# Attention and a mixture of experts on one core: stores on GpSimd's queue, and seven smaller edits

## The chip, the core and the metric

The kernel runs on one core of a Trainium2 chip. A core has a matrix engine (TensorE, PE in the profile, with its weight loads as PEld), a vector engine (VectorE, DVE), an engine for activations and copies (ScalarE, ACT), GpSimd (POOL) and SyncE (SP), which here only issues DMAs. Each engine works through its own instructions in order and waits for the others at semaphores; a "q" behind an engine's name (POOLq) means its sequencer. Sixteen DMA engines move data between the device memory and the core's own memory. The metric is the device time of one execution in microseconds (us).

## What is computed

The first half is sparse attention over 8 batches, 8 heads, 576 positions and 64 columns a head. The second half sends each of the 4,608 rows through one of 8 experts.

```python
# attention: heads 0-3 see the last 32 positions, heads 4-7 see positions of their own class mod 32
scores = scale * np.matmul(q, k.transpose(0, 1, 3, 2))
...
scores = np.where(masks[None, :, :, :], scores, -1000000000.0)
...
x = attn_out.transpose(0, 2, 1, 3)    # to (8, 576, 512)
# experts
logits = np.einsum('bsd,de->bse', x, w_gate)
local_gate = 1.0 / (1.0 + np.exp(-np.einsum('bsd,de->bse', x, w_local).squeeze(-1)))
...
            fresh_e = int(np.argmax(logits[b, s]))
            if s == 0 or local_gate[b, s] < 0.5:
                e = fresh_e
            else:
                e = prev_e if prev_e >= 0 else fresh_e
...
            h = np.maximum(x[b, s] @ w1[e], 0.0)
            out[b, s] = p[e] * (h @ w2[e])
```

`p` is the softmax of the logits. `w1` is 512 x 1024 and `w2` is 1024 x 512 for each expert, so that one expert's weights are 4 MB.

## The kernel before

**Attention** (`attention`, L146). The work is cut into 32 steps' worth of head pairs: 8 batches of 4 pairs, two local ones (0 and 1) and two strided ones (2 and 3). A pair is two units. The loop at L431 is a schedule written out by hand; nothing reorders it. At step n it issues, in this order: the load of the pair four steps ahead (SP), the scores of pair n with their exponentials (PE, ACT) and, for a local pair, the multiplication by `maskL` (DVE); the stores of finished rows; `turn_x` of pair n-2 (transposes on PE, copies on ACT); `values` and `norm` of pair n-1 (PE, then DVE, which reads PSUM and writes the normalized rows `xl` or `xs`); and then what hangs on the batch. With `last` the number of a batch's last pair, `logits` follow at `last + 2`, `gates` at `last + 4` (at `last + 3` for batches 3 and 7) and `store_p`, the probabilities' store, at `last + 5`. A strided pair's scores begin with a matrix product that adds `maskS` (L256), made at the start by `classes` out of two index tables each.

`store_x` (L303) issues two DMAs for a batch's two local pairs and ten for its two strided ones; `store_p` two more. All are on SP's queue, which also holds the loads, in the order of the schedule. The tiles `xl`, `xs` and `xT` have two buffers each, so that a norm waits for the stores of two batches ago.

**Router.** After four batches `router.steps` and `router.table` work out which rows go to which expert. They hang in `also`, a list of extra calls for each step. The table took seven calls (where, what, three groups of lanes, products, numbers), one a step from step 24; the gathers of the first expert's rows are issued by POOL at step 30, and scaled by ACT at the end of step 31. `products` and `logits` both use the PSUM tile `tps`, of which there is one.

**Experts** (`Experts.run`, L768). Each expert's rows come in units of 256 (a pair of tiles), 128 (`single`) or 64 (`half`). A pair is multiplied with fewer products by sums of weight blocks (`Weights.sums`, DVE) and sums of rows (`row_sums`, DVE). The first expert's weights and sums fall in the attention: `W[0].ready` at step 6 issues both 2 MB loads at once, and from step 9 two sums are made a step. A `half` (L912) forms its hidden rows with one accumulation, applies relu on ACT, transposes the next unit's rows, transposes its own hidden rows, copies these from PSUM with one DVE instruction (L927), and multiplies by `w2` (L934). Gathers and scatters are indirect DMAs from POOL (L736 and L762).

**The end.** A count `redo` of rows that did not fit, or of sums out of range, decides at L123 whether everything is computed again by `general`; with these inputs it is not. The branch is stated with `preferred_fallthrough_block=False`.

Of the kernel before, what the change touches and what calls it, by code (L numbers as in the profile page):

```python
# [18 lines left out]
P = 128  # L19
# [31 lines left out]
RB = 4  # L51
# [47 lines left out]
@with_exitstack  # L99
def attention_then_scomoe(ctx: ExitStack, tc: tile.TileContext, qkl, qks, vl, vs, wg, q, k, vl2, vs2, wg2, w1, w2, out):  # L100
    nc = tc.nc
    dram = ctx.enter_context(tc.tile_pool(name="dram", bufs=1, space=DRAM))
    xd = dram.tile([N, DX], F32, name="xd")
    xg = dram.tile([N, D], F32, name="xg")
    keep = ctx.enter_context(tc.tile_pool(name="keep", bufs=1))
    ident = keep.tile([P, P], F32, name="ident")
    make_identity(nc, ident)

    with ExitStack() as fast:
        once = fast.enter_context(tc.tile_pool(name="once", bufs=1))  # L110
        router = Router(once, tc, ident)
        one = Weights(once)
        spot = (once.tile([P, 2, DX], F32, name="x0"), once.tile([P, 2, DK, P], F32, name="xt"),
                once.tile([P, 4, 2, P], F32, name="tt"))
        with tc.manual_schedule():
            moe = Experts(nc, tc, xd, w1, w2, out, ident, router, one, spot)
            with ExitStack() as part:
                attention(part, tc, qkl, qks, vl, vs, wg, xd, ident, router, moe)
            with ExitStack() as part:
                redo = moe.run(part)  # L120


    with tc.If(redo > 0, preferred_fallthrough_block=False):  # L123
        with ExitStack() as slow:
            general(slow, tc, q, k, vl2, vs2, wg2, w1, w2, xg, out, ident)
# [20 lines left out]
def attention(ctx, tc, qkl, qks, vl, vs, wg, xd, ident, router, moe):  # L146
# [42 lines left out]
    nc.vector.tensor_copy(identb, ident)  # L189

# [9 lines left out]
    def classes(n, c):  # L200
        i = consts.tile([GK, n], I32, name=f"i{n}")
# [3 lines left out]
        for mult, pattern in ((1, [[0, n]]), (0, [[1, n]])):  # L205

            nc.gpsimd.iota(i, pattern=pattern, base=0, channel_multiplier=mult)
            t = consts.tile([GK, n], F32, name=f"cls{n}{mult}")
# [10 lines left out]
        if n == GK:  # L219
            nc.vector.tensor_copy(maskS[:, 0:2 * n].rearrange("p (a x) -> p a x", a=2), across(cls, [n, 2, n]))  # L220
        else:
            nc.vector.tensor_copy(maskS[:, 2 * GK:], cls)
    classes(GK, GC)
# [79 lines left out]
    def store_x(u):  # L303
# [3 lines left out]
        for a in range(2):  # L307
            if u.local:
                w = LQ // 2
                o = dst.rearrange("(t a p) d -> a p t d", a=2, p=w)[a]  # L310
                nc.sync.dma_start(out=o, in_=src[a * (P - w):a * (P - w) + w])
                continue
            for j in range(GT):
# [3 lines left out]
                nc.sync.dma_start(out=o, in_=src[a * (P - w):a * (P - w) + w, j])  # L317
# [22 lines left out]
    def logits(b):  # L340
# [3 lines left out]
        for a, c in ((0, slice(0, n)), (1, slice(n, S))):  # L344
            for kk in range(DK):
# [6 lines left out]
        nc.scalar.copy(out=o[:, :, 0:GC * (GT - 1)].rearrange("p y (j c) -> p j y c", c=GC),  # L352
                       in_=ps[64:, 0, 0:n].rearrange("p (j y c) -> p j y c", j=GT - 1, c=GC))
# [37 lines left out]
    def store_p(b):  # L391
        dst = xd[b * S:(b + 1) * S, D:DX]
        full = S // P
        nc.sync.dma_start(out=dst[0:full * P].rearrange("(t p) c -> p t c", p=P), in_=probs[:, 0:full, b])
        nc.sync.dma_start(out=dst[full * P:], in_=probs[0:S - full * P, full, b])
# [17 lines left out]
    also[0] = [lambda: classes(GL, GR)]  # L413
# [13 lines left out]
    also[m + 6].append(lambda: moe.gather(moe.first))  # L427
# [3 lines left out]
    for n in range(len(units) + 3):  # L431
        if n < len(units):
            if n + ahead < len(order):
                load(*order[n + ahead])
            if n == 6:
                steps = moe.W[0].ready(nc, w1=moe.w1, w2=moe.w2, e=0)
# [16 lines left out]
        for do in steps[:2] if n >= 9 else []:  # L453
            do()
            steps.remove(do)
        for b in range(B):
            last = PAIRS * b + PAIRS - 1
            if n == last + (3 if b in (RB - 1, B - 1) else 4):
                gates(b)
            if n == last + 5 and b < B - 1:  # L460
# [11 lines left out]
class Router:  # L472
# [107 lines left out]
    def table(self, r, bank, rooms):  # L580
# [66 lines left out]
        return [where, what, some(0, 8), some(8, 16), some(16, n), products, numbers]  # L647
# [32 lines left out]
class Weights:  # L680
# [11 lines left out]
    def load(self, nc, w1, w2, e):  # L692
        nc.sync.dma_start(out=self.w1, in_=w1[e].rearrange("(k p) f -> p k f", p=P))
        nc.sync.dma_start(out=self.w2, in_=w2[e].rearrange("(k p) f -> p k f", p=P))

    def ready(self, nc, w1, w2, e):
        self.load(nc, w1, w2, e)
        return self.sums(nc.vector)
# [28 lines left out]
class Experts:  # L727
# [40 lines left out]
    def run(self, ctx):  # L768
# [143 lines left out]
        def half(r, w, nxt, steps):  # L912
# [9 lines left out]
            relu(h.rearrange("p k x -> p (k x)"), a)  # L922
            self.turn(nxt, bank)
# [3 lines left out]
            nc.vector.tensor_copy(ht, ps)  # L927
# [4 lines left out]
            for f in range(FK):  # L932
                for g in range(2):
                    nc.tensor.matmul(b[g * HALF:(g + 1) * HALF, 0:256], lhsT=ht[:, f % 4, f // 4 * HALF:(f // 4 + 1) * HALF],  # L934
                                     rhs=w.w2[:, f, g * 256:(g + 1) * 256], start=(f == 0), stop=(f == FK - 1),
# [76 lines left out]
        where, what, lanes1, lanes2, lanes3, products, numbers = router.table(1, bank, rooms)  # L1012
        places[2] += slots(sums, [2])[0]
        places[3] += slots(sums, [2])[0]
        places += [[where], [what], [lanes1] + slots(sums, [1])[0], [lanes2] + slots(sums, [1])[0], [lanes3] + slots(sums, [2])[0]]
# [32 lines left out]
        output(second, W[e % 2], pair_hidden(second, W[e % 2], [[check]]), None, [])  # L1048
# [3 lines left out]
def shifted_attention(ctx, tc, q, k, vl, vs, wg, xd, ident, probs, codes):  # L1052
# [121 lines left out]
    def store_x(b, grp):  # L1174
# [4 lines left out]
        nc.sync.dma_start(out=dst, in_=src)  # L1179
# [333 lines left out]
```

## Time and profile before

Three runs took 706.05, 709.14 and 708.79 us, a median of 708.79. The profiled execution took 709.35 us, of which the span from the first to the last instruction is 707.5.

| Stage | us | what is in it |
|---|---|---|
| 0 to 7 | 7 | constants, warm-up products, first loads |
| 7 to 172 | 165 | attention, the router for four batches; PE busy 156.5, DMA share 0.78 |
| 172 to 192 | 20 | last batch's rows and gates, the first expert pair begins |
| 192 to 691 | 499 | experts; PE busy 491.9 |
| 691 to 707.5 | 16.5 | last scatters, the branch, the end |

The page has one line for each DMA queue (packets, MB, share of 16 engines), and one for each group of DMAs by line:

```profile
q1 hardware_dynamic: 34480, 74.06, 30.4%
q0 software_dynamic: 6144, 19.72, 8.7%
xd<-xl SPq DMA_DIRECT2D x16, 288.0 KB
xd<-xs SPq DMA_DIRECT2D x64, 63.0 KB
```

The first queue is SP's, the second POOL's. Queries by line give each instruction's duration: minimum, median and maximum in nanoseconds, then the first and last start. A stage's windows give each engine's busy time in it, and the TensorE clock granted there.

### The profile page before, as it was taken

The page shows a single profiled execution, that of the slowest core. Times are in us where ns is not written, and L with a number is a line of the kernel's source. Part 1 is how long each engine was busy: PE and PEld are TensorE (multiplying, and loading weights), DVE is VectorE, ACT ScalarE, POOL GpSimd, SP SyncE. Part 2 cuts the span into 40 slices and gives each one's busy share as a digit, 9 for nine tenths or more (in the row PEclk, how much of TensorE's full clock was granted, in tenths as well). Part 3 has the DMA queues.
Part 4 walks back from the last instruction along what each step waited for, and adds up shares of the span by engine and source line. Part 5 has one row for each costly group of instructions (what it writes and reads, how often), then busy time and mean ns, then how long its engine had stood idle before and what let it go on. Part 6 is the DMA issues. An engine that isn't in the chain of part 4 may idle for free. (4 is left out here: it accounts for less than half of the span.)

```text
span 707.5 us, 14841 instructions
## 1 busy us (share of the span) xinstructions
PE 672.4 (95%) x6057; PEld 579.5 (82%) x6058; DVE 358.6 (51%) x830; ACT 198.0 (28%) x361; POOL 91.9 (13%) x105
## 2 busy tenths in 40 slices
PE   8999999989999999999999999999999999999990
PEld 5887788876998999769988999996799999697690
DVE  6666767663887345414631654651255565331130
ACT  3553444534232122123121222222222221211210
POOL 3000000002011211211211202202011211111101
PEclk9999999889999999999999999999999999999996
DMA  9897777864701145162217118111711711111000
GB/s 325 297 343 255 260 272 265 282 181 112 261 27 36 61 138 182 38 213 82 79 47 252 47 35 299 46 34 38 255 50 48 270 42 57 37 51 39 24 2 33
DMA packets 41324, 95.79 MB, mean 135 GB/s; under 512 B 8782, under 2 KB 17998, under 8 KB 41152
## 3 DMA queue, kind: packets, MB, share of 16 engines
q1 hardware_dynamic: 34480, 74.06, 30.4%
q0 software_dynamic: 6144, 19.72, 8.7%
q8 instruction: 66, 1.08, 0.6%
q14 instruction: 106, 0.87, 0.4%
q10 hardware_dynamic: 528, 0.07, 0.1%
HBM read 74.66 MB, written 19.69 MB: 133 GB/s over the span
## 5 line engine op out<-in xcount | busy, mean ns | idle before, releaser
L762 POOL DMA_INDIRECT out_dram<-y,tab x40 | 46.0, 1151 | 373.0 <-DVE y L794 266.9
L806 PE MATMUL lps<-tt,ws 128*128 128x128 f32 x768 | 91.7, 276 | 0.0
L806 PEld LDWEIGHTS lps<-tt,ws 128*128 128x128 f32 x768 | 88.5, 192 | 0.3
L842 PE MATMUL mps<-wt,k 128*128 128x256 f32 x384 | 85.6, 379 | 0.0
L842 PEld LDWEIGHTS mps<-wt,k 128*128 128x128 f32 x384 | 72.9, 190 | 9.9
L736 POOL DMA_INDIRECT x<-xd,gi x40 | 40.3, 1008 | 219.7 <-ACT e L266 151.7
L806 PE MATMUL lps<-xt,w1t 128*128 128x128 f32 x512 | 63.0, 276 | 3.0 <-ACT y L940 1.9
L806 PEld LDWEIGHTS lps<-xt,w1t 128*128 128x128 f32 x512 | 60.4, 192 | 6.5 <-ACT y L940 3.7
L794 DVE TENSOR_TENSOR h<-lps,u 128x512 f32<-128x512 f32 x48 | 33.1, 690 | 60.9 <-PE lps L806 60.7
L842 PE MATMUL mps<-w2t,h 128*128 128x256 f32 x256 | 60.6, 380 | 0.7 <-ACT q L858 0.7
L266 ACT ACTIVATE e<-sps 128x576 f32<-128x576 f32 (+1 forms) x64 | 41.2, 650 | 51.1 <-PE sps L262 48.5
L262 PE MATMUL sps<-qk 64*128 64x96 f32 (+2 forms) x704 | 52.1, 287 | 1.6 <-DMA qk<-in_qks_dram 1.5
L842 PEld LDWEIGHTS mps<-w2t,h 128*128 128x128 f32 x256 | 47.3, 190 | 6.8 <-ACT q L858 1.1
L262 PEld LDWEIGHTS sps<-qk 64*128 64x128 f32 (+2 forms) x704 | 44.0, 190 | 9.6 <-issue 6.1
L793 ACT ACTIVATE h<-h 128x512 f32<-128x512 f32 x48 | 30.3, 630 | 71.1 <-DVE h L794 69.2
L793 ACT ACTIVATE h<-lps 128x512 f32<-128x512 f32 x28 | 16.5, 594 | 83.3 <-PE lps L806 67.0
L794 DVE TENSOR_TENSOR u<-lps,p 128x512 f32<-128x512 f32 x16 | 11.1, 691 | 53.7 <-PE lps L806 33.3
L742 ACT ACTIVATE x<-x 128x512 f32<-128x512 f32 (+1 forms) x40 | 27.1, 718 | 35.0 <-DMA x<-xd,gi 21.1
L750 ACT COPY xt<-xps 128x512 f32<-128x512 f32 (+1 forms) x38 | 19.9, 565 | 48.2 <-PE xps L749 48.1
L927 DVE COPY h<-lps 128x512 f32<-128x512 f32 x4 | 2.8, 692 | 56.4 <-PE lps L926 56.4
L806 PE MATMUL lps<-tt,w1t 128*128 128x128 f32 x256 | 31.3, 275 | 0.0
L806 PE MATMUL lps<-xt,ws 128*128 128x128 f32 x256 | 31.3, 275 | 0.0
(221 smaller groups left out, 986.5 us busy)
## 6 DMA issues: line engine op xcount, KB each, us to landing
w1t<-in_w_dram SPq DMA_DIRECT2D x8, 2048.0 KB
w2t<-in_w_dram SPq DMA_DIRECT2D x8, 2048.0 KB
qk<-in_qkl_dram SPq DMA_DIRECT2D x16, 592.0 KB
qk<-in_qks_dram SPq DMA_DIRECT2D x16, 576.0 KB
vl<-in_vf_dram SPq DMA_DIRECT2D x8, 780.0 KB
vs<-in_vg_dram SPq DMA_DIRECT2D x8, 639.8 KB
xd<-xl SPq DMA_DIRECT2D x16, 288.0 KB
xd<-xs SPq DMA_DIRECT2D x64, 63.0 KB
```

What stands on the lines that cost most here:

```text
L262: nc.tensor.matmul(ps[0:m, h, c:c + w], lhsT=t[r, S + j * width:S + j * width + m], rhs=t[r, j * width:j * width + w], start=(u.local and ...
L266: nc.scalar.activation(e[0:kb, :, 0:n], ps[0:kb, :, 0:n], Act.Exp, bias=0.0, scale=1.0 / DH ** 0.5)
L736: self.nc.gpsimd.indirect_dma_start(out=r.x[0:r.m, i], out_offset=None, in_=self.xd[0:r.rows], in_offset=bass.IndirectOffsetOnAxis(ap=r.gi ...
L742: self.nc.scalar.activation(r.x[0:r.m, i, 0:D], r.x[0:r.m, i, 0:D], Act.Copy, scale=r.gate[i][0:r.m])
L750: self.nc.scalar.copy(out=r.xt[:, i, :, 0:r.m], in_=ps[:, :, 0:r.m])
L762: s = self.nc.gpsimd.indirect_dma_start(out=self.out, out_offset=bass.IndirectOffsetOnAxis(ap=r.si[i][0:r.m], axis=0), in_=y[0:r.m, i], in ...
L793: relu = lambda o, i: nc.scalar.activation(o, i, Act.Relu)
L794: add = lambda o, i, p: nc.vector.tensor_tensor(o, p, i, op=Alu.add)
L806: nc.tensor.matmul(ps[:, f], lhsT=m[:, kk, f * P:(f + 1) * P], rhs=v[:, kk], start=(start and f == 0 and kk == 0), stop=(kk == 1), skip_gr ...
L842: nc.tensor.matmul(ps[:, 0:256], lhsT=m[:, f], rhs=v[:, f], start=(start and f == 0), stop=(f == 3), skip_group_check=True)
L927: nc.vector.tensor_copy(ht, ps)
```

## The change

All stores of normalized rows and probabilities go from SP's queue to POOL's. Besides: the two index tables of each mask are made first on POOL, and both masks before the first scores; the first expert's weights come in eight DMAs of 0.5 MB at steps 5 to 12, with the sums from step 10; `gates` follow at `last + 3` and `store_p` at `last + 4` for every batch; the router's table takes six calls, and the gathers are issued at step 29; the strided copy of the last batch's logits is DVE's instead of ACT's; `half` shares its relu and its copy between ACT and DVE, puts half of the next unit's transposes between its own transposes and their use, and takes the products in another order; and the branch at the end has a label and, ahead of the last output, a hint for four engines that it is likely taken. The fallback `general` has one store moved too, which is not run.

```diff
-    with tc.If(redo > 0, preferred_fallthrough_block=False):
+    with tc.If(redo > 0, label="redo"):
...
+    count = {}
+    for n in (GK, GL):
+        for mult, pattern in ((1, [[0, n]]), (0, [[1, n]])):
+            count[n, mult] = consts.tile([GK, n], I32, name=f"i{n}{mult}")
+            nc.gpsimd.iota(count[n, mult], pattern=pattern, base=0, channel_multiplier=mult)
...
-    def classes(n, c):
-        i = consts.tile([GK, n], I32, name=f"i{n}")
+    for n, c in ((GK, GC), (GL, GR)):
...
-            nc.gpsimd.iota(i, pattern=pattern, base=0, channel_multiplier=mult)
-            t = consts.tile([GK, n], F32, name=f"cls{n}{mult}")
+            i, t = count[n, mult], consts.tile([GK, n], F32, name=f"cls{n}{mult}")
...
             if u.local:
...
-                nc.sync.dma_start(out=o, in_=src[a * (P - w):a * (P - w) + w])
+                nc.gpsimd.dma_start(out=o, in_=src[a * (P - w):a * (P - w) + w])
...
-                nc.sync.dma_start(out=o, in_=src[a * (P - w):a * (P - w) + w, j])
+                nc.gpsimd.dma_start(out=o, in_=src[a * (P - w):a * (P - w) + w, j])
...
-        nc.scalar.copy(out=o[:, :, 0:GC * (GT - 1)].rearrange("p y (j c) -> p j y c", c=GC),
-                       in_=ps[64:, 0, 0:n].rearrange("p (j y c) -> p j y c", j=GT - 1, c=GC))
+        copy = nc.scalar.copy if b < B - 1 else nc.vector.tensor_copy
+        copy(out=o[:, :, 0:GC * (GT - 1)].rearrange("p y (j c) -> p j y c", c=GC),
+             in_=ps[64:, 0, 0:n].rearrange("p (j y c) -> p j y c", j=GT - 1, c=GC))
...
-        nc.sync.dma_start(out=dst[0:full * P].rearrange("(t p) c -> p t c", p=P), in_=probs[:, 0:full, b])
-        nc.sync.dma_start(out=dst[full * P:], in_=probs[0:S - full * P, full, b])
+        nc.gpsimd.dma_start(out=dst[0:full * P].rearrange("(t p) c -> p t c", p=P), in_=probs[:, 0:full, b])
+        nc.gpsimd.dma_start(out=dst[full * P:], in_=probs[0:S - full * P, full, b])
...
-    also[0] = [lambda: classes(GL, GR)]
...
-    also[m + 6].append(lambda: moe.gather(moe.first))
+    also[m + 5].append(lambda: moe.gather(moe.first))
...
-            if n == 6:
-                steps = moe.W[0].ready(nc, w1=moe.w1, w2=moe.w2, e=0)
+            if 5 <= n < 13:
+                moe.W[0].load(nc, moe.w1, moe.w2, 0, n - 5)
+            if n == 10:
+                steps = moe.W[0].sums(nc.vector)
...
-            if n == last + (3 if b in (RB - 1, B - 1) else 4):
+            if n == last + 3:
                 gates(b)
-            if n == last + 5 and b < B - 1:
+            if n == last + 4 and b < B - 1:
                 store_p(b)
...
-        return [where, what, some(0, 8), some(8, 16), some(16, n), products, numbers]
+        return [where, what, some(0, 8), some(8, n), products, numbers]
...
+    def load(self, nc, w1, w2, e, piece=None):
...
+        if piece is None or piece < DK:
+            c = slice(0, DK) if piece is None else slice(piece, piece + 1)
+            nc.sync.dma_start(out=self.w1[:, c], in_=w1[:, c])
+        if piece is None or piece >= DK:
+            c = slice(0, FK) if piece is None else slice(2 * (piece - DK), 2 * (piece - DK) + 2)
+            nc.sync.dma_start(out=self.w2[:, c], in_=w2[:, c])
...
             h, ht = u("h22", hs), u("h12", hs)
-            relu(h.rearrange("p k x -> p (k x)"), a)
-            self.turn(nxt, bank)
+            flat = h.rearrange("p k x -> p (k x)")
+            relu(flat[:, 0:256], a[:, 0:256])
+            nc.vector.tensor_scalar(flat[:, 256:], a[:, 256:], 0.0, None, Alu.max)
+            self.turn(nxt, bank, 0)
             ps = psl.tile(hs, F32, name="lps")
             for f in range(4):
                 nc.tensor.transpose(ps[:, f], h[:, f], self.ident)
-            nc.vector.tensor_copy(ht, ps)
+            nc.vector.tensor_copy(ht[:, 0:2], ps[:, 0:2])
+            nc.scalar.copy(out=ht[:, 2:], in_=ps[:, 2:])
+            self.turn(nxt, bank, 1)
...
-            for f in range(FK):
+            for i, f in enumerate((0, 4, 1, 5, 2, 6, 3, 7)):
...
-        output(second, W[e % 2], pair_hidden(second, W[e % 2], [[check]]), None, [])
+        h = pair_hidden(second, W[e % 2], [[check]])
+        tc.mark_branch_hint_location("redo", "LikelyTaken", ENG)
+        output(second, W[e % 2], h, None, [])
```

More of the change, by code (lines that the diff above doesn't have):

```diff
@@ L204, in classes @@
         both = []
-        for mult, pattern in ((1, [[0, n]]), (0, [[1, n]])):
-            nc.gpsimd.iota(i, pattern=pattern, base=0, channel_multiplier=mult)
-            t = consts.tile([GK, n], F32, name=f"cls{n}{mult}")
+        for mult in (1, 0):
+            i, t = count[n, mult], consts.tile([GK, n], F32, name=f"cls{n}{mult}")
             nc.vector.tensor_copy(t, i)
@@ L218, in classes @@
                                 channel_multiplier=-1)
[L219 to L223, printed above, removed]
+        count[n] = cls
+    n = GK
+    nc.vector.tensor_copy(maskS[:, 0:2 * n].rearrange("p (a x) -> p a x", a=2), across(count[n], [n, 2, n]))
+    nc.vector.tensor_copy(maskS[:, 2 * n:], count[GL])
     fold = consts.tile([P, E + 1], F32, name="fold")
@@ L452, in attention @@
             busy(FILL)
-        for do in steps[:2] if n >= 9 else []:
+        for do in steps[:2]:
             do()
@@ L690, in __init__ @@
         self.b = {11: b[:, 0:4, 0:256], 12: b[:, 0:4, 256:], 21: b[:, 4:8, 0:256], 22: b[:, 4:8, 256:]}
[L692 to L698, printed above, removed]
+    def load(self, nc, w1, w2, e, piece=None):
+        w1, w2 = w1[e].rearrange("(k p) f -> p k f", p=P), w2[e].rearrange("(k p) f -> p k f", p=P)
+        if piece is None or piece < DK:
[4 more added lines that the diff above has]
+            nc.sync.dma_start(out=self.w2[:, c], in_=w2[:, c])
     def sums(self, engine):
@@ L931, in half @@
             b = u("mps0", [P, 512], psm)
-            for f in range(FK):
+            for i, f in enumerate((0, 4, 1, 5, 2, 6, 3, 7)):
                 for g in range(2):
                     nc.tensor.matmul(b[g * HALF:(g + 1) * HALF, 0:256], lhsT=ht[:, f % 4, f // 4 * HALF:(f // 4 + 1) * HALF],
-                                     rhs=w.w2[:, f, g * 256:(g + 1) * 256], start=(f == 0), stop=(f == FK - 1),
+                                     rhs=w.w2[:, f, g * 256:(g + 1) * 256], start=(i == 0), stop=(i == FK - 1),
                                      skip_group_check=True)
@@ L1011, in run @@
         places = slots(router.steps(1, bank), [2, 2, 1, 1])
-        where, what, lanes1, lanes2, lanes3, products, numbers = router.table(1, bank, rooms)
+        where, what, lanes1, lanes2, products, numbers = router.table(1, bank, rooms)
         places[2] += slots(sums, [2])[0]
         places[3] += slots(sums, [2])[0]
-        places += [[where], [what], [lanes1] + slots(sums, [1])[0], [lanes2] + slots(sums, [1])[0], [lanes3] + slots(sums, [2])[0]]
+        places += [[where], [what], [lanes1] + slots(sums, [1])[0], slots(sums, [2])[0], [lanes2] + slots(sums, [1])[0]]
         output(self.first, W[0], pair_hidden(self.first, W[0], places), other, places)
@@ L1178, in store_x @@
                dst.rearrange("(p c) d -> p c d", c=ST))
-        nc.sync.dma_start(out=dst, in_=src)
+        nc.gpsimd.dma_start(out=dst, in_=src)
     def turn_x(b, pair):
```

## The prediction

> **What bounds the kernel now.** I read the first part of the page, then TensorE's (PE) waits, then the clock, then the end of the span.
>
> ```profile
> PE 672.4 (95%) x6057; PEld 579.5 (82%) x6058; DVE 358.6 (51%) x830; ACT 198.0 (28%) x361; POOL 91.9 (13%) x105
> PEclk9999999889999999999999999999999999999996
> ```
>
> PE is the bound. By the stage windows its work ends at 691.0 of 707.5 us, so 16.5 us are tail and 691.0 - 672.4 = 18.6 us are gaps. Nothing that leaves PE as it is pays more than these, save the clock. TensorE's waits name the gaps (total, times, longest):
>
> ```profile
> PE mps L934 <- DVE h L927: 3.1, 4, 0.8
> PE vps L364 <- DVE sums L299: 1.9, 5, 0.7
> PE tps L630 <- DVE lT L354: 1.9, 1, 1.9
> PE sps L262 <- DMA qk<-in_qks_dram: 1.5, 1, 1.5
> PE vps L364 <- DVE lT L354: 1.4, 1, 1.4
> PE tps L327 <- DVE sums L299: 0.9, 1, 0.9
> PE sps L256 <- ACT e L266: 0.7, 1, 0.7
> ```
>
> Only the first line lies in the experts; the rest are in the attention stage (7 to 178 us). There the granted clock also fell to half four times (windows: PE busy, PEld, DVE, ACT, POOL, clock, DMA share, GB/s):
>
> ```profile
> 57.58:60.99 3.41, 3.41 (x44) 2.95 (x42) 0.34 (x2) 1.35 (x2) 0.00 (x0) 0.50 0.89 317
> 122.43:129.26 6.83, 6.83 (x75) 6.21 (x75) 3.82 (x13) 2.00 (x4) 0.00 (x0) 0.50 0.77 237
> 146.32:149.74 3.42, 3.42 (x47) 2.97 (x47) 3.32 (x9) 1.28 (x3) 0.00 (x0) 0.50 0.97 280
> 156.56:159.98 3.42, 3.42 (x30) 2.68 (x27) 0.27 (x1) 0.00 (x0) 0.00 (x0) 0.50 0.22 67
> ```
>
> PE counts as busy in them. The timeline shows the price: L286 2.16 or 2.44 us for 1.39, L262 2.82 for 1.58; summed, some 7.5 us. The first window follows the 1.5 us wait for qk, the last the 1.9 us wait at L630.
>
> The tail, from the instructions by line (duration min/median/max, first and last start):
>
> ```profile
> L976 POOLq INC_SWDGE_SEM  x8: 510/1120/1738, 262.6 to 666.6; - x8
> L123 POOLq INC_SWDGE_SEM  x1: 1787/1787/1787, 695.7 to 695.7; - x1
> L123 POOLq COMPARE_BRANCH  x2: 48/52/56, 692.0 to 697.6; - x2
> L1509 POOLq DRAIN  x3: 44/112/6699, 700.0 to 707.3; - x3
> ```
>
> The last scatter starts at 692.26. GpSimd (POOL) waits for its landing till 695.7, counts semaphores 1.79 us, branches at 697.6, begins the drain only at 700.0, and drains 6.70 us. The tail is POOL's alone.
>
> **What the Trainium skill says.** "DMA: Bandwidth & Descriptors", SWDGE vs HWDGE vs iDMA: a DMA from GpSimd has its descriptors written by software on that engine. The page agrees: GpSimd's queue is software_dynamic, SyncE's (SP) hardware_dynamic. Same page, Issuing engines are not separate DMA queues: all issue into the same 16 engines, and another issuer saves issue time alone. No run here shows that yet. "Runtime: NRT & Kernel Launch", Instruction fetch mechanics: a taken branch out of the fetched window waits for a fetch. The trace agrees: 2.4 us from POOL's branch to the next instruction. "TensorE: Matmul & The Clock Gate", What's actually happening: idle windows of about 3.4 us halve the clock. The windows above are 3.4 and 6.8 us long, though PE was not wholly idle before them.
>
> **The change part by part**, against the profiled execution's own 709.35 us (707.5 of span and 1.85 around it; the runs' median is 708.79).
>
> (1) Masks first. Before, the second mask's 12 DVE operations run from 9.9 to 13.3 us, before the second pair's maskL multiplication (13.2); PE waits 0.7 at L256 (12.70 to 13.36) and 0.85 at L327 (14.61). After, all iotas lead POOL's queue, and DVE's two chains (24 operations of 0.2 to 0.29, two casts of 0.47 and 0.21: 6.6 us after identb's end at 2.6) end near 9.2. That is past 8.55, where the first multiplication starts now, so values(0) comes 0.7 later; 1.5 goes. Net -0.8.
>
> (2) Weights in eighths, steps 5 to 12. The same 4 MB, but no burst: before, DMA share is 1.0 from 40 to 60 us with both weights issued at 36.4, and qk arrives late. Spread at 0.5 MB a step, and with SP free of its xs stores (about 9.5 us of issue each batch), loads issue earlier. The wait goes: -1.5. Of its clock window (1.5 us lost), half: -0.8. The sums start a step later (10), two steps after w1's last piece is issued: no stall priced.
>
> (3) Gates one step earlier. The five L364 waits on L299 are at the strided step, behind a norm which first waits for the xs stores of two batches ago (L300 on DMA xd<-xs, 1.4 us in 5). Gates of batch 3, already a step earlier, waited nothing. -1.5 of 1.9. DVE's work in the earlier step rises by some 2.2 us, that of the next falls by as much.
>
> (4) The table takes six steps, not seven, so the products leave the step whose logits hold the only tps buffer: -1.9 at L630, and half of its 1.5 us of clock, -0.8. DVE's last two lane groups share a step (3 x 0.64 us), covered by the lighter step after (3).
>
> (5) Halves. Now a half's PE waits 0.78 for one 0.69 us copy (L927). After, two engines copy halves (0.42 on DVE; 0.37 on ACT behind an xt copy of 0.58) while PE does four more transposes (0.55), and the first four products need only DVE's part. relu on two engines frees 0.2 more. Four halves x 0.75: -3.0. The 0.47 at the next unit (L806 on L940) stays.
>
> (6) Hint. POOL's 2.4 us between branch and drain: -2.4. Even if the hint fails, a branch taken once at 692.0 misses under the scatter's 3.4 us landing. Bounds 0 and -2.6.
>
> (7) Last batch's lT copy on DVE: two handovers fewer of L354's 1.4 us wait, -0.3.
>
> (8) Stores on POOL: 112 DMAs more (10 + 2 + 2 a batch). No row of before is a plain store from POOL. Nearest is L736, 0.97 us with 0.30 us between two; scatters of 64 rows take 0.93, of 128 some 1.0, about 1.2 ns a row, so 63-row xs stores 0.95 and 288-row xl stores 1.2 are estimates. 14 x 1.3 = 18.2 us a batch against 165 / 8 = 20.6: it fits, narrowly. Queued behind them on POOL are the gathers: the first two now follow ten stores (about 13 us, issue at step 29, landing 3.6 later), needed by ACT at the end of step 31 some 16.5 us on: +0.5. Those for `other` (now 168.7) come near 184; ACT scales at 199.65: slack. Bounds 0 and +3. The other cost is the end. INC_SWDGE_SEM grew from 0.51 us after 14 DMAs to 1.79 after 80, 19 ns for each ever issued, so nothing was retired. If the drain walks the same entries it costs 6.70 / 80 = 84 ns each. With 192: +2.2 and +9.3, the upper bound +11.5. The skill's "SBUF — State Buffer", SBUF size, gives descriptors 16 KiB of scratch per partition; at its 16 bytes each that is an estimated 1,024 per ring. The stores overrun this, so old entries must retire. With about 28 of the stores left beside the 80: +0.5 and +2.3, taken as +2.8. Lower bound -4, if a full ring is cleared whole.
>
> Sum: -0.8 - 2.3 - 1.5 - 2.7 - 3.0 - 2.4 - 0.3 + 0.5 + 2.8 = -9.7; 709.35 - 9.7 = **699.6 us**, 1.3% under the median.
>
> **Rivals.** A: nothing retires, the end grows by 11.5, not 2.8: 708.3. For: the 19 ns line never bent in 80. Against: the scratch. B, the slow side: POOL's queue overruns. From 1.47 us a store (20.6 / 14) it falls behind, and the gathers for `other` wait for every store. At 1.7 us: 112 x 1.7 = 190 us from 19 us on, 209; gathers and landing 216.5, against about 192.5 needed: +24, 724. For: 1.3 is close to 1.47[...]. Against: the 1.2 ns a row. C: the attention's gaps move instead of going, since DVE's order is full (its 10 us windows reach 8.9): (2), (3) and (4) give nothing, 709.35 - 3.2 = 706.2.
>
> **Numbers.** Likeliest 0.62 (its own range 694 to 704), A 0.14, B 0.13, C 0.11. Within 0.5% is what a measurement cannot tell from no change: 705.2 to 712.3. A and C fall mostly there. Range 692.5 to 708.5: low, (8) at -4 with more clock back; high, A. B stays out. Faster 0.69, same 0.16, slower 0.15.
>
> **What would show it.** Right: L934's wait near 0, no wait at L630 and for qk, POOL's drain 30 to 40% longer with no 2.4 us before it, xd stores on POOL of 0.95 to 1.2 us. Wrong: stores over 1.47 us, a drain of 16 us, ACT's L742 waiting at 190 us, or DVE waits on xd larger than 1.6 us.

## The result, and the profile after

The changed kernel takes 698.88 us, the median of four runs (698.04 to 699.77); four runs of the kernel before beside them had a median of 707.42. The ratio is 0.989, with a 95% interval of 0.984 to 0.994. The profiled execution took 699.77 us, with a span of 698.1, against 709.35 and 707.5 before: 9.6 us less, where 9.7 were forecast. The sum hit; of its parts several did not, and the errors cancelled. That they cancel to 0.1 us is luck: the four runs alone lie 1.7 us apart.

The page of the changed kernel, engine totals, granted clock by fortieths of the span, and the group of the strided stores (line, engine, operation, out<-in, count; busy us, mean ns; idle time before):

```profile
PE 670.3 (96%) x6058; PEld 577.4 (83%) x6058; DVE 361.3 (52%) x835; ACT 198.1 (28%) x364; POOL 160.5 (23%) x217
...
PEclk9999999998999999999999999999999999999996
...
L319 POOL DMA_DIRECT2D xd<-xs x80 | 46.8, 589 | 44.4 <-DVE sums L301 36.3
```

PE is still the bound. POOL went from 91.9 to 160.5 us busy, and none of TensorE's waits below is put down to it: a strided store costs POOL 0.59 us, where the prediction took 0.95 and set the limit at 1.47.

TensorE's waits in the changed kernel (total us, times, longest):

```profile
PE vps L367 <- DVE sums L301: 2.3, 7, 0.6
PE lps L812 <- ACT y L950: 1.9, 4, 0.5
...
PE vps L367 <- DVE lT L357: 1.3, 1, 1.3
PE lps L812 <- issue: 1.1, 2, 0.6
PE tps L329 <- DVE lT L357: 1.1, 2, 0.7
...
```

Set beside the list of before (L364 is now L367, L299 is L301, L630 is L634, L934 is L944): the copies' wait of 3.1 us in the half units, the 1.9 us at the codes' transposes, the 1.5 us for qk and the 0.7 us at L256 are gone. The waits of the gates for the norm's reciprocal are not; they went from 1.9 us in 5 to 2.3 in 7. The 1.9 us at L812 stood before too (at L806). In all, the gaps between PE's matmuls fell from 17.4 to 10.2 us by their modelled ends; the 17.4 are the prediction's 18.6 without the 1.3 us before PE's first matmul.

The clock fell to half in two windows inside the work (same columns as in the windows of before):

```profile
75.29:78.70 3.41, 3.41 (x39) 2.95 (x38) 0.86 (x6) 1.35 (x2) 1.35 (x2) 0.50 1.00 316
167.45:174.27 6.82, 6.82 (x36) 6.77 (x36) 2.76 (x15) 0.82 (x2) 2.74 (x4) 0.50 0.47 154
```

That is 10.2 us at half clock for 17.1 before. What a window costs can be read from profiles below with the same matmuls as the changed kernel. Two with 3.4 us of it had PE's end at 679.4 and 679.9 us, three with 10.2 us at 681.9 to 682.4: 2.5 us for 6.8, or 0.37 us for each. The 74 runs of the kernel before that stand beside the experiments say the same: time at half clock, worked out from each run's mean granted clock, goes with 0.39 us of run time for each. So the clock gave about 2.5 us of the gain between the two profiles.

GpSimd's end, by line (durations min/median/max in ns, first and last start in us). INC_SWDGE_SEM is the instruction with which POOL counts the semaphores of its DMAs:

```profile
L986 POOLq INC_SWDGE_SEM  x8: 940/1570/2186, 254.8 to 657.4; - x8
L123 POOLq COMPARE_BRANCH  x1: 69/69/69, 682.9 to 682.9; - x1
L123 POOLq INC_SWDGE_SEM  x1: 2228/2228/2228, 686.5 to 686.5; - x1
L1521 POOLq DRAIN  x3: 40/109/8404, 688.8 to 697.8; - x3
```

The last counting takes 2.23 us for 1.79, the drain 8.40 for 6.70, and between the two lies nothing, where before a branch and 2.4 us without an instruction lay. The branch comes earlier now, at 682.9. Apart from the last scatter (683.1), POOL's next instruction after it comes at 685.5, before the last landing that POOL waits for (686.5), so the branch costs nothing at the end. The tail after PE's end is 16.2 us (681.9 to 698.1) for 16.5: the two sizes that grew and the one that went cancel.

### The profile page after: what moved, and what is told of

It reads as the page before. It is cut to its first block, busy times and chain, and to the rows that moved or that the text cites. A ratio compares the mean times of both kernels' runs of the same rounds, so it can differ in the third digit from the quotient of the medians.

```text
span 698.1 us, 14861 instructions
## 1 busy us (share of the span) xinstructions
PE 670.3 (96%) x6058; PEld 577.4 (83%) x6058; DVE 361.3 (52%) x835; ACT 198.1 (28%) x364; POOL 160.5 (23%) x217
## 4 chain that ended last, share of the span: by engine, by line
PE 87%; DVE 8%; DMA 1%; issue 1%; ACT 1%; POOL 0%; POOLq 0%; DVEq 0%
PE lps L812 29%; PE mps L848 27%; PE vps L288 5%; PE sps L264 4%; PE lps L903 4%; PE mps L914 4%; PE tps L329 3%; PE xps L755 2%; PE mps L944 2%; PE lps L924 2%; PE vps L367 1%; DMA xd<-xl 1%; PE sps L258 1%; PE tps L348 1%; DVE xl L302 1%
## 5 line engine op out<-in xcount | busy, mean ns | idle before, releaser
L812 PE MATMUL lps<-tt,ws 128*128 128x128 f32 x768 | 92.7, 277 | 0.0
L812 PEld LDWEIGHTS lps<-tt,ws 128*128 128x128 f32 x768 | 89.7, 194 | 0.2
L812 PE MATMUL lps<-xt,w1t 128*128 128x128 f32 x512 | 64.9, 281 | 3.0 <-ACT y L950 1.9
L812 PEld LDWEIGHTS lps<-xt,w1t 128*128 128x128 f32 x512 | 62.0, 196 | 6.5 <-ACT y L950 3.7
L319 POOL DMA_DIRECT2D xd<-xs x80 | 46.8, 589 | 44.4 <-DVE sums L301 36.3
L264 PE MATMUL sps<-qk 64*128 64x96 f32 (+2 forms) x704 | 50.3, 280 | 0.1
L264 PEld LDWEIGHTS sps<-qk 64*128 64x128 f32 (+2 forms) x704 | 42.3, 183 | 8.1 <-issue 7.0
L799 ACT ACTIVATE h<-lps 128x512 f32<-128x512 f32 (+1 forms) x28 | 15.6, 563 | 81.8 <-PE lps L812 65.6
L748 ACT ACTIVATE x<-x 128x512 f32<-128x512 f32 (+1 forms) x40 | 27.1, 717 | 34.7 <-DMA x<-xd,gi 21.2
L812 PE MATMUL lps<-tt,w1t 128*128 128x128 f32 x256 | 31.3, 275 | 0.0
L812 PE MATMUL lps<-xt,ws 128*128 128x128 f32 x256 | 31.3, 275 | 0.0
```

The source lines that it names most:

```text
L264: nc.tensor.matmul(ps[0:m, h, c:c + w], lhsT=t[r, S + j * width:S + j * width + m], rhs=t[r, j * width:j * width + w], start=(u.local and ...
L319: nc.gpsimd.dma_start(out=o, in_=src[a * (P - w):a * (P - w) + w, j])
L799: relu = lambda o, i: nc.scalar.activation(o, i, Act.Relu)
L812: nc.tensor.matmul(ps[:, f], lhsT=m[:, kk, f * P:(f + 1) * P], rhs=v[:, kk], start=(start and f == 0 and kk == 0), stop=(kk == 1), skip_gr ...
```

## The experiments

All ratios are to the kernel before, run on the same chip beside the experiment; from the third row on its median there was 709.1 to 710.9 us. TensorE's end, the end after it and the time at half clock are those of the profiled execution.

| Kernel | Median, us | Ratio, interval | PE's end | rest of span | half clock | last count, drain |
|---|---|---|---|---|---|---|
| before | 707.42 | 1 | 691.0 | 16.5 | 17.1 | 1.79, 6.70 |
| changed | 698.88 | 0.989, 0.984 to 0.994 | 681.9 | 16.2 | 10.2 | 2.23, 8.40 |
| stores back on SP | 700.99 | 0.988, 0.984 to 0.992 | 685.0 | 13.9 | 10.2 | 1.77, 6.61 |
| no hint | 700.06 | 0.986, 0.982 to 0.990 | 682.1 | 16.1 | 10.2 | 2.22, 8.40 |
| gates late | 698.44 | 0.985, 0.981 to 0.989 | 679.9 | 16.1 | 3.4 | 2.23, 8.40 |
| half of the stores on GpSimd | 695.72 | 0.980, 0.976 to 0.984 | 689.3 | 9.9 | 20.5 | 1.03, 3.50 |
| eight DMAs more | 697.58 | 0.982, 0.979 to 0.985 | 682.4 | 16.4 | 10.2 | 2.29, 8.66 |
| two batches on GpSimd | 704.65 | 0.991, 0.988 to 0.994 | 689.1 | 17.0 | 20.5 | 2.33, 8.89 |
| own tiles in the halves | 701.84 | 0.987, 0.983 to 0.991 | 679.4 | 16.3 | 3.4 | 2.23, 8.40 |
| before, with stores on GpSimd | 707.20 | 0.995, 0.993 to 0.997 | 684.1 | 18.5 | 3.4 | 2.22, 8.48 |
| six stores more, two banks | 687.33 | 0.968, 0.965 to 0.971 | 681.1 | 7.5 | 13.7 | 0.49, 1.30 |
| whole weights, old branch | 701.15 | 0.989, 0.986 to 0.992 | 680.2 | 18.5 | 6.8 | 2.22, 8.48 |
| table in seven steps | 707.07 | 0.994, 0.992 to 0.996 | 690.2 | 16.1 | 17.1 | 2.23, 8.40 |
| four more, banks, gates late | 687.59 | 0.969, 0.966 to 0.973 | 679.9 | 7.2 | 10.2 | 0.45, 1.14 |

The runs of one kernel spread by up to 7 us (the kernel before by 8.6), mostly with the time at half clock, so a difference of 1 or 2 us between two medians decides nothing here; the waits in the traces decide, with one execution of each kernel.

**Stores back on SP.**

```diff
-                nc.gpsimd.dma_start(out=o, in_=src[a * (P - w):a * (P - w) + w])
+                nc.sync.dma_start(out=o, in_=src[a * (P - w):a * (P - w) + w])
...
```

> All stores of rows and gates back on SP's queue, the rest as in the changed kernel. My theory: the stores on GpSimd cost at the end only, in the counting of semaphores and in the drain. So the drain returns from 8.40 to 6.7 us and the last counting from 2.23 to 1.79, and the kernel comes out 1 to 2 us faster than the changed one (about 697.5), unless SP's queue then holds a load up. Rival: freeing SP's queue is what made the loads early and took the two waits of TensorE away (1.5 us for qk, 1.9 us at the codes' transposes); then the wait for qk is back and the time is 2 us or more over the changed kernel (701 or more).

The end is as said, 1.77 us for the counting and 6.61 us for the drain:

```profile
L123 POOLq INC_SWDGE_SEM  x1: 1768/1768/1768, 689.6 to 689.6; - x1
...
L1521 POOLq DRAIN  x3: 40/109/6613, 691.4 to 698.6; - x3
```

But PE ends 3.2 us later than in the changed kernel at the same time at half clock, so the kernel is not faster: my expectation of 697.5 failed, and the medians don't tell the two apart. The rival failed in its reason as well. The wait for qk of the strided pairs is not back (0.5 us in two), nor the one at the codes' transposes; the loss lies in a wait of 1.8 us at L329 for ScalarE's copy and one of 1.5 us at L367 for the norm. Another 0.7 us is a wait for the first loads, which comes and goes between profiles. The two other kernels with half of the stores or more on SP (below) agree: PE's gaps from 140 to 185 us sum to 4.8 or 4.9 us in these three, and to 2.3 to 3.1 in the kernels that have all stores on GpSimd and the change's six-step table. So the stores on GpSimd gain 2 to 3 us in the attention and cost 2.3 at the end: in sum they are worth little here.

**No hint.**

```diff
-        tc.mark_branch_hint_location("redo", "LikelyTaken", ENG)
```

> The branch hint alone is left out, the branch around the fallback keeps its new form. My theory: the 2.4 us before the drain went because GpSimd's branch is now taken at the end of its work (2.6 us of missing instructions beside the last scatter's landing of 3.4 us), and the hint adds nothing: same time as the changed kernel, within 0.5 us, and GpSimd's branch again followed by some 2.6 us. Rival: the hint is what saved it; then 2 us or more slower, with a gap of 2.4 us between the last counting of semaphores and the drain.

As the theory says: 700.06 us; the branch is at 683.2, the drain follows the counting at once (686.8 plus 2.2, then 689.0). The hint does nothing that shows. The other half of that edit is tried further below.

**Gates late.**

```diff
-            if n == last + 3:
+            if n == last + (3 if b in (RB - 1, B - 1) else 4):
                 gates(b)
-            if n == last + 4 and b < B - 1:
+            if n == last + 5 and b < B - 1:
                 store_p(b)
```

> The gates and the store of the gates back at their old steps, the rest as in the changed kernel. Prediction: 1.5 us slower, since the five waits of 1.9 us for the norm's reciprocal come back. My theory now: those waits (2.3 us in 7 in the changed kernel) are for the norm that frees the accumulator and stand wherever the gates are; within 0.5 us of the changed kernel, with the waits for the reciprocal between 1.5 and 2.5 us in both.

The waits on the reciprocal are 1.9 us in 6 here, against 2.3 in 7 with the early gates, and the time is no longer than that of the step without the hint beside it (698.44 against 700.06, at a mean granted clock of 0.986 against 0.984 over the runs). Moving the gates gained nothing that shows.

**Half of the stores on GpSimd.**

```diff
+    store = lambda b: nc.gpsimd if b < B // 2 else nc.sync
...
-                nc.gpsimd.dma_start(out=o, in_=src[a * (P - w):a * (P - w) + w])
+                store(u.b).dma_start(out=o, in_=src[a * (P - w):a * (P - w) + w])
...
```

> Stores of batches 0 to 3 on GpSimd, of batches 4 to 7 on SP, the rest as in the changed kernel: 56 stores on GpSimd where the changed kernel has 112. Two theories for the small growth of the end. One: the descriptors' room fills once, after some 89 DMAs, and all older entries are cleared; then 136 - 89 = 47 are left at the end, the last counting takes 0.24 + 47 x 0.0194 = 1.15 us and the drain 0.18 + 47 x 0.0815 = 4.0 us, and the kernel is 5 us faster than the changed one (about 694). Two: nothing is ever cleared, and a plain store costs a fifth of an indirect DMA (3.8 ns in the counting, 15 ns in the drain); then counting 2.0 us, drain 7.55 us, about 1 us faster at most.

The first theory. The counting rises to 2.13 us after 96 DMAs, is 0.47 us after 107, and ends at 1.03 us; the drain is 3.50:

```profile
L988 POOLq INC_SWDGE_SEM  x8: 472/1316/2126, 262.1 to 664.9; - x8
...
L123 POOLq INC_SWDGE_SEM  x1: 1030/1030/1030, 693.8 to 693.8; - x1
...
L1523 POOLq DRAIN  x3: 44/109/3504, 694.9 to 699.0; - x3
```

A median in the first line that lies above the last counting can only come from a fall within the run. Both durations give the number of entries left: (1.03 - 0.24) / 0.0194 = 41 and (3.50 - 0.18) / 0.0815 = 41. So entries do get cleared, 95 of them between two countings that lie 11 DMAs apart, and a plain store weighs what an indirect DMA weighs: after 70 DMAs, 56 of them stores, the counting took 1.63 us, and 0.24 + 70 x 0.0194 is 1.60. The median is the lowest up to here, though PE's end is late in the profiled execution (20.5 us at half clock, and waits of 1.7, 1.5 and 1.2 us in the attention that the changed kernel lacks).

**Eight DMAs more, and two batches on GpSimd.** The large store of the gates in two parts; and the rule of the step before with `b < 2`.

```diff
-        nc.gpsimd.dma_start(out=dst[0:full * P].rearrange("(t p) c -> p t c", p=P), in_=probs[:, 0:full, b])
+        for t in range(0, full, 2):
+            nc.gpsimd.dma_start(out=dst[t * P:(t + 2) * P].rearrange("(t p) c -> p t c", p=P), in_=probs[:, t:t + 2, b])
```

> The changed kernel with each batch's large store of gates split in two: 200 DMAs on GpSimd, not 192, and nothing else. My theory: DMA number 97 clears all entries whose transfer has landed, and number 193 would again; the changed kernel stops one DMA short of it. So here the entries are cleared eight DMAs before the end, some 8 to 12 are left: the last counting falls from 2.23 to about 0.45 us, the drain from 8.40 to about 1.0 us, and the kernel is 7 to 9 us faster than the changed one, about 690.5. Rival: room is a matter of bytes or descriptors and the second clearing is far off; then eight entries more, counting 2.4, drain 9.1 us, some 1 us slower.

> Stores of batches 0 and 1 alone on GpSimd, the other six on SP: 28 + 80 = 108 DMAs. If DMA number 97 clears, some 12 are left at the end: counting about 0.5 us, drain about 1.2 us, against 2.23 and 8.40 in the changed kernel. TensorE's part is then as with all stores on SP (end of its work some 2 to 3 us later than in the changed kernel at the same clock); in all 5 to 7 us faster than the changed kernel. Rival (room in bytes or descriptors, of which the large stores take more than the gathers): no clearing within 108; counting 2.3 us, drain 9 us, slower than the changed kernel.

Both theories of a count failed. With 200 DMAs nothing is cleared a second time, and with 108 nothing at all:

```profile
L123 POOLq INC_SWDGE_SEM  x1: 2332/2332/2332, 694.0 to 694.0; - x1
```

This is the line of the kernel with two batches; (2.33 - 0.24) / 0.0194 = 108 entries, all that were ever issued. In the kernel with 200, the counting after 134 DMAs (1.00 us) says 39 left, so 95 had been cleared; in the changed kernel after 126 (0.94 us) it says 36, so 90. The six smaller stores ahead moved the number and not the place, which is batch 6 in both. These places are worked out from the countings, on the view that a clearing takes all that was issued before it. What fills is then not the number of DMAs; that it is their content, rows or descriptors, is put to the test further below.

**Own tiles in the halves.**

```diff
-            h, ht = u("h22", hs), u("h12", hs)
+            h, ht = [u(n, hs) for n in ("h22", "h12")], [u(n, hs) for n in ("h11", "h21")]
...
-            relu(flat[:, 0:256], a[:, 0:256])
-            nc.vector.tensor_scalar(flat[:, 256:], a[:, 256:], 0.0, None, Alu.max)
+            relu(flat[0][:, 0:256], a[:, 0:256])
+            nc.vector.tensor_scalar(flat[1][:, 256:], a[:, 256:], 0.0, None, Alu.max)
...
```

> In the half units, each engine's half of the relu and of the copy goes to a tile of its own; the operations, their engines and their order stay. In the changed kernel the two halves run one after the other (relu: ScalarE 0.39 us, then VectorE 0.42 us; copy: VectorE 0.42 us, then ScalarE 0.37 us), each waiting for the other's semaphore, and a half unit takes 9.22 us, only 0.35 less than before. Theory: they wait because they write one tile; with two tiles they run beside each other, a half unit takes 8.4 to 8.6 us, and four of them give 2.4 to 3.2 us. Rival: they wait because they read one bank of the accumulator; then nothing changes.

What had to be explained is this stretch of the changed kernel's timeline (start us, duration, engine, line; in brackets the idle time and its releaser):

```profile
296.94 0.39 ACT L799 ACTIVATE h<-lps 128x256 f32<-128x256 f32 x1 [1.78 <-PE lps L924]
297.35 0.42 DVE L930 TENSOR_SCALAR h<-lps 128x256 f32<-128x256 f32 x1 [14.74 <-ACT h L799]
...
297.83 0.20 PEld L934 LDWEIGHTS lps<-ident,h 128*128 128x128 f32 x2 [0.26 <-DVE h L930]
...
298.31 0.42 DVE L935 COPY h<-lps 128x256 f32<-128x256 f32 x1 [0.53 <-PE lps L934]
...
298.76 0.37 ACT L936 COPY h<-lps 128x256 f32<-128x256 f32 x1 [0.61 <-DVE h L935]
```

VectorE begins its half of the relu when ScalarE has ended, and ScalarE its half of the copy when VectorE has. The two halves of the relu take 0.81 us so, where the kernel before took 0.60 for the whole:

```profile
304.75 0.60 ACT L793 ACTIVATE h<-lps 128x512 f32<-128x512 f32 x1 [1.78 <-PE lps L918]
```

With tiles of their own the order is the same, and so is the half unit, 9.23 us from its first product to its last:

```profile
294.21 0.38 ACT L799 ACTIVATE h<-lps 128x256 f32<-128x256 f32 x1 [1.78 <-PE lps L924]
...
294.63 0.42 DVE L930 TENSOR_SCALAR h<-lps 128x256 f32<-128x256 f32 x1 [14.73 <-ACT h L799]
```

The theory fell: it is not the tiles that they write. The rival, that it is the bank they read, is tried below.

**Before, with the stores on GpSimd.** The kernel before, with `nc.sync` replaced by `nc.gpsimd` in `store_x` and `store_p` and nothing else.

> The kernel before with nothing changed but the stores of rows and gates, all on GpSimd: the headline of the change alone. From the step with all stores on SP (701.0 against 698.9 for the changed kernel, with the end 2.1 us shorter and TensorE's end some 3 us later) I expect TensorE's end 3 us earlier than in the kernel before, the wait for qk gone, the last counting at 2.2 and the drain at 8.4 us: about 1 us faster than before, not told apart from no change. Rival: the stores on GpSimd carry most of the gain; then 5 us or more faster.

The ratio is 0.995, with an interval that excludes 1: 3.7 us, between the two. The end is as expected, counting 2.22 and drain 8.48 us with 2.6 us after the old branch. The 1.5 us wait for the strided qk at 57 us is gone here, with the weights still in two bursts. But PE's gaps are not smaller in sum (17.3 us for 17.4): 0.9 us less up to 185 us, 0.9 more in the experts. In the traces the gain lies in PE's busy time (665.5 us for 672.4), some 5 us of it by the price above for 3.4 us at half clock in place of 17.1, and over the runs the mean granted clock is 0.982 against 0.979. The headline edit alone gives between a third and a half of what the whole change gives, and by the traces it gives it mostly through the clock; why its runs have less half clock is not shown.

**Six stores more, and two banks.** Six stores that nothing reads, in the last expert's last unit; and in the half units the products, and then the transposes, each go to two banks, with own tiles for the halves and all products of the first bank ahead of those of the second.

```diff
+            moe.pad = dram.tile([6, 512, PW], F32, name="pad")
...
+        fill = lambda i: nc.gpsimd.dma_start(out=self.pad[i].rearrange("(t p) c -> p t c", p=P),
+                                             in_=self.router.probs[:, 0:4, i])
...
-            a = psl.tile(hs, F32, name="lps").rearrange("p k x -> p (k x)")
+            a = [psl.tile(hs, F32, name="lps").rearrange("p k x -> p (k x)")[:, 0:256] for _ in range(2)]
+            for c in range(2):
...
-            ps = psl.tile(hs, F32, name="lps")
+            ps = [u(f"mps{i}", [P, 512], psm)[:, 0:256].rearrange("p (k x) -> p k x", k=2) for i in (1, 2)]
...
```

> Two edits that show in different places. First, in the last expert's last unit GpSimd issues six more stores of 512 rows of 64 bytes, into a scratch tensor that nothing reads; nothing is left out. The step with 200 DMAs showed that it is not the count that clears the entries: the first clearing stayed at the same store of batch 6, with six more DMAs ahead of it, so it follows the rows. By the rows the changed kernel ends some 700 to 2,000 rows short of a second clearing; 3,072 more rows reach it. Theory: 4 to 10 entries are left, the last counting takes 0.3 to 0.45 us for 2.23, the drain 0.5 to 1.0 us for 8.40, and the kernel is 8 to 9 us faster. Rival: no second clearing; counting 2.35, drain 8.9 us. Second, in the half units the first products go to two banks, the transposes too, and each engine's half has a tile of its own. Theory: the relu's two halves waited for each other because of the one bank they read (own tiles alone changed nothing); with two banks the VectorE half starts without ScalarE's semaphore, ScalarE's half lies beside the second bank's products, and a half unit takes 8.6 to 8.9 us instead of 9.22. Rival: the waits come from elsewhere, and it stays at 9.2.

Both theories held in kind. The end, by line:

```profile
L124 POOLq INC_SWDGE_SEM  x1: 492/492/492, 685.9 to 685.9; - x1
...
L1527 POOLq DRAIN  x3: 40/109/1299, 686.5 to 688.3; - x3
```

Of 198 entries 13 are left by the counting and 14 by the drain, where 4 to 10 were expected, and the rest of the span after PE is 7.5 us for 16.2. The half unit:

```profile
299.34 0.42 DVE L933 TENSOR_SCALAR h<-lps 128x256 f32<-128x256 f32 x1 [14.36 <-PE lps L927]
299.61 0.47 PEld L937 LDWEIGHTS mps<-ident,h 128*128 128x128 f32 x4
...
300.20 0.42 DVE L938 COPY h<-mps 128x256 f32<-128x256 f32 x1 [0.44 <-PE mps L937]
300.45 0.38 ACT L939 COPY h<-mps 128x256 f32<-128x256 f32 x1
```

VectorE's relu now waits for PE alone, the copies overlap, and the four transposes follow in one piece. For the copies the bank is the cause: their engines, sizes and order are those of the step with own tiles. For the relu the order of the products changed too, so that ScalarE's half lies beside the second bank's products; the two are not told apart. From its first product to its last a half takes 8.74 us, as forecast, against 9.23 in the changed kernel and 9.57 before. To the next unit's first product it is 9.20, 9.69 and 10.04 us.

**Whole weights and the old branch.**

```diff
-            if 5 <= n < 13:
-                moe.W[0].load(nc, moe.w1, moe.w2, 0, n - 5)
-            if n == 10:
+            if n == 6:
+                moe.W[0].load(nc, moe.w1, moe.w2, 0)
+            if n == 9:
                 steps = moe.W[0].sums(nc.vector)
...
-    with tc.If(redo > 0, label="redo"):
+    with tc.If(redo > 0, preferred_fallthrough_block=False):
...
```

> Two parts of the change undone that show in different places: the first expert's weights in two loads at the seventh step, as before, and the branch around the fallback in its old form without the hint. Prediction for the weights: a wait for qk of about 1.5 us and a window of half clock after it come back, 2.3 us. Rival: with the stores off SP's queue the wait stays away (under 0.5 us) whatever the size of the loads. Prediction for the branch: the 2.4 us between the last counting of semaphores and the drain come back, all on the path. Rival: under 0.3 us, since the code's order around it has changed.

For the weights the rival holds: no wait for qk between 40 and 60 us (gaps of 0.28 us there in all, as in the changed kernel). The 1.2 us of waiting for qk that the trace has lies in the first 20 us, at the start of the program, where the weights are not yet being loaded. For the branch the prediction holds:

```profile
L123 POOLq COMPARE_BRANCH  x2: 42/48/54, 681.2 to 686.9; - x2
L123 POOLq INC_SWDGE_SEM  x1: 2224/2224/2224, 684.6 to 684.6; - x1
...
L1520 POOLq DRAIN  x3: 44/112/8476, 689.4 to 698.4; - x3
```

A second branch is back after the counting, at 686.9, and the drain begins 2.5 us later.

**Table in seven steps.**

```diff
-        return [where, what, some(0, 8), some(8, n), products, numbers]
+        return [where, what, some(0, 8), some(8, 16), some(16, n), products, numbers]
...
-    also[m + 5].append(lambda: moe.gather(moe.first))
+    also[m + 6].append(lambda: moe.gather(moe.first))
...
```

> The table in seven steps again, and with it the first gathers one step later; the rest as in the changed kernel. Prediction: TensorE's wait of 1.9 us at the codes' transposes (or at the transposes that take the one accumulator instead of it) comes back, with half a window of clock 2.7 us in all. Rival: the accumulator's last user is no longer the table once the gates are earlier, and the wait stays away; then the same time as the changed kernel within 0.5 us.

The wait at the codes' transposes is back with 1.9 us, and a second one of 2.6 us with it:

```profile
PE tps L329 <- ACT xT L333: 2.6, 1, 2.6
...
PE tps L634 <- DVE lT L357: 1.9, 1, 1.9
```

The second comes by way of ScalarE. The first gathers start at 162.4 and 165.1 us; ScalarE comes to its scaling of their rows (L748) early and stands 3.4 and 2.0 us until they land, and its copy that frees the one accumulator of the transposes is queued behind. PE ends 8.3 us later than in the changed kernel: 4.5 us of gaps, some 2.5 for 6.8 us more at half clock, and a rest of about 1.3 that I have not traced. Without the clock that is 5.8 us, so beside the stores on GpSimd the edit is worth twice its forecast or more.

**Four more, banks, gates late.** As the step with six, with four stores, and the gates as in the step with late gates.

> The step with six more stores and two banks, with four more stores instead of six, and the gates back at their old steps. With six, 13 entries were left of 198, so 185 had been cleared. Theory: a clearing spares the last eight DMAs and came at the third of the six stores (number 193); then it comes with four as well, 196 - 185 = 11 are left, the last counting takes about 0.45 us and the drain about 1.1 us, and the time is that of the step with six within 1 us (687). Rival: it came at the fifth or sixth; then four don't reach it, counting 2.3 us, drain 8.7 us, some 9 us slower. For the gates: no difference in either.

687.59 us; counting 0.453 and drain 1.136 us, 11 and 12 entries left. Four stores reach the clearing, as forecast, and the gates again make no difference. So 196 DMAs reach a second clearing where 200 without these 2,048 rows more did not: what fills is the content. This and the step with six are the fastest kernels of the study, 2% under the changed one by their ratios.

## Why the prediction was right, part by part

(8) The stores. Their cost at the end was sized well: +0.44 in the counting and +1.70 in the drain, +2.1 in all, for +2.8. The reason given, that old entries must retire and some 28 stores stay beside the 80, was right in kind: they were cleared once, by the countings in batch 6, and some 102 entries were left at the end (22 beside the 80). The room for them was an estimate from the Trainium skill (16 KiB from "SBUF — State Buffer", SBUF size; the 16 bytes a descriptor stand in "DMA: Bandwidth & Descriptors", Terms), and no run here confirms its size or its unit: about 90 stores go in before the first clearing, or 108 DMAs of which 80 are indirect, without one. Where the room ends in rows or bytes stays open. The stores' price on POOL was more than twice too high: the four groups of stores take 68.2 us, 8.5 a batch, for 18.2. So rival B, the overrun from 1.47 us, was never near. Two of the signs named ahead did not come: the drain grew by 25%, not 30 to 40, and a store took 0.59 us, not 0.95 to 1.2. What the part left out is the gain of 2 to 3 us in the attention, which the step with stores back on SP shows beside the other edits; in the kernel before, the stores alone left PE's gaps as they were in sum.

(6) The branch: -2.4 forecast, 2.4 to 2.5 measured by putting it back, and the clause "even if the hint fails" is the one that came true. The edit's name is the hint; its effect is where the branch lies.

(4) The table: -2.7 forecast. The wait at L630 was real; the wait for the gathers that it would have dragged along was missed, since its cost was put into part (8) as +0.5.

(1) Masks: -0.8 forecast. The first batch's logits start at 28.4 us for 29.7, and the waits at L256 and L327 that the part named are gone. It was not run alone, and in eight of the eleven other profiles with the same masks a wait of 0.3 to 1.4 us for the first loads stands in the first 20 us.

(5) Halves: -3.0 forecast, -1.4 measured (10.04 to 9.69 us, four times). The copies did what was forecast: TensorE's wait of 0.78 us is gone, with 0.42 us on VectorE ahead of the first products. The step "relu on two engines frees 0.2 more" failed: the halves share a bank and ran one after the other, 0.39 and 0.42 us in sequence where it was one of 0.60 us. So 0.2 us was lost where 0.2 was to be won, the size of the 0.4 us that a half lacks. With two banks the same idea gives 4 x 0.84 = 3.4 us.

(3) Gates: -1.5 forecast, nothing measured. I took the wait for one on a norm that was itself late through the stores of two batches ago. The stores' wait is gone (VectorE waits 1.2 us in 4, all on the local stores), and the gates still wait: the norm reads the accumulator whose buffer they take, and that order is the same in either step.

(2) Weights: -2.3 forecast. The wait for qk went, but the eighths were not needed for it. Whole loads with the stores on GpSimd have no such wait, in the kernel before as in the changed one, and the stores on SP with the loads in eighths have little of it (0.5 us in two). Each of the two edits is enough; the part could not be added to one of them.

(7) The last copy: -0.3 forecast, not seen (L357's waits 1.3 and 1.1 us for 1.4 and 0.9).

The clock gave 2.5 us where 1.6 had been counted in (2) and (4). So (3), (5) and (7) were 3.4 us too hopeful, and the attention's gain from the stores, (1), (4) and the clock made up for it. Rival A, with nothing retired, is excluded by the countings; rival C, that the attention's gaps only move, by the gaps.

## What to carry to other kernels

Before an end-of-kernel drain is taken as given, read how the counting of GpSimd's DMA semaphores grows through the run: here it named the entries left to within one or two, and four stores of 512 short rows, issued while GpSimd was idle, took 9 us off a tail in which GpSimd alone still works. When an operation is split over two engines, give each half its own bank of the accumulator, and look in the timeline whether the second half's releaser is the first. Two edits that remove the same wait should be priced once, and a wait should be followed to what the buffer is held by before it is put down to the last thing that its holder waited for.

## What the runs showed of the hardware

- The counting of semaphores follows 0.24 us + 19.4 ns an entry, and GpSimd's last drain 0.18 us + 81.5 ns an entry, from 11 entries (0.45 and 1.14 us) to 108 (2.33 and 8.89 us), for plain stores as for indirect DMAs. The number is known for 14 to 80 entries (the kernel before) and for 108 (two batches); elsewhere it is read back from the line, and the two durations agree to within two.
- Entries are cleared many at a time, not as their transfers land: 90 in the changed kernel, 95 in two others (half of the stores, eight DMAs more), none in the one with 108 DMAs. The step with four more stores fits a clearing that spares the last eight DMAs (11 left, as forecast), which no other run tests.
- A plain store from GpSimd occupies it 0.58 us (63 or 64 rows), 0.66 us (288 rows) or 0.78 us (512 rows of 64 bytes), with no pause between two until the ninth or tenth strided store of a batch: in the first four batches this one waited 0.9 to 1.8 us, mostly for the landing of an earlier one. An indirect DMA of up to 128 rows takes some 1.0 to 1.2 us on average, with 0.3 us before a second one.
- Windows at half clock of 3.4 us or twice that come while PE counts as busy. Their places differ between kernels with the same matmuls in the same order (75 and 167 us in the changed kernel; 94, 115 and 170 us in the one without the hint; 113 us in the one with own tiles). In all 14 traces they start on a grid of 3.413 us: the two of the changed kernel lie 27 times that apart. The grid's offset from the program's start differs from execution to execution, and where it is nearly the same, so are most places (10.9, 96.2 and 116.7 us with half of the stores, two batches and six stores more). In every grid interval just before a half-clock window PE had stood idle 0.28 us or more. Of more than 2,400 intervals at full clock with less than 0.2 us idle none was followed by one, of the 312 others 40 were. So short gaps count, and which of them do was not found.
